# mLSTM cell and squared-ReLU FFN on one core: chunks 5 and 6 in 64x64 quarters, FFN2 of the first group ahead of FFN1 of the third

## The chip, the cores and the metric

One Trainium2 chip, one of its cores. The kernel is one launch; its time is the device time of that core in microseconds (us), given as the median of several runs. The engines are named as the profile names them: PE (TensorE, matmuls; PEld its weight loads), DVE (VectorE), ACT (ScalarE), POOL (GpSimd) and SP (SyncE, which only issues DMAs). All data are float32.

## The reference

Two blocks follow each other. The first is an mLSTM cell: for each of 4 batches and 8 heads a state C (40 x 40) and n (40) is carried over 768 steps of time. The second is a feed-forward network (FFN) with a squared ReLU on the 3072 x 320 result.

```python
batch, n_heads, seq, head_dim = (4, 8, 768, 40)
for t in range(S):
    m_new = np.maximum(f_gate[:, :, t] + m, i_gate[:, :, t])
    f_stab = np.exp(f_gate[:, :, t] + m - m_new)
    i_stab = np.exp(i_gate[:, :, t] - m_new)
    C = f_stab[..., None, None] * C + i_stab[..., None, None] * np.einsum('bhd,bhe->bhde', vt, kt)
    n = f_stab[:, :, None] * n + i_stab[:, :, None] * kt
    h_tilde = np.einsum('bhde,bhe->bhd', C, qt)
    nq = np.einsum('bhd,bhd->bh', n, qt)[:, :, None]
    denom = np.maximum(np.abs(nq), 1.0)
    y[:, :, t] = o * h_tilde / denom            # o = sigmoid(o_gate)
x = attn_out.transpose(0, 2, 1, 3).reshape(3072, 320)
h = np.maximum(x @ w_in, 0.0)                   # w_in 320 x 2048
out = (h * h) @ w_out                           # w_out 2048 x 320
```

## The kernel before

**Chunks.** Time is cut into chunks of 128 steps: 6 for a batch (NB), 24 in all (NT), numbered s = 0 to 23, c = s mod 6 within the batch. "Chunk 5" in the title is s=4, "chunk 6" s=5, "chunk 7" s=6, "chunk 8" s=7; below, and in the prediction, a chunk is named by s. Within a chunk the recurrence is turned into matmuls: scores k q^T (`scores`), weighted by exponentials of the gates (`weigh`, ACT, eight exponentials a chunk, L511; the causal mask is an affine select on POOL, `mask`, L469/L475), times the values (with a column of ones, so that the denominator comes along), plus the old state times q with its decay; the state C of the next chunk is the old one decayed plus k^T times weighted v. Two chunks make a group g of 256 rows for the FFN (12 groups, NG).

**Two forms of the attention.** For s < X_SQ = 6 `attend` works with full 128x128 tiles: old state times q (`hi`, L622), the state's update (`dC`, L634), weighted scores times values (`hp`, L645); then DVE puts them together, and `normalise` (L805 to 818) divides. The 128 rows of x must be turned for the FFN: `turn_rows` (L843 to 853) does it with two transposes (L848) and four half ones (L850) on PE and one ACT copy (L853). From s = 6 on `attend_begin` and `attend_end` do the same products in 64x64 quarters of PE (`values_of_C` L708, `values_of_P` L727, `new_C` L738), in two halves: the first in `attend_begin`, the second in `attend_end`, with a tiny DVE operation (L700) between them that the second half waits for. The numerators come out turned; DVE transposes 32x32 squares of them (L758), they are stored to DRAM (`store_num`, L773) and loaded again in the other order (`load_num`, L778, four DMAs), DVE scales (`normalise_turned`, L790 to 803), the rows are stored (`store_rows`, L828), loaded (`load_rows`, L833, four DMAs) and transposed in squares on DVE (`turn_squares`, L840). k and q are turned likewise by `pair_up` (to DRAM), `load_squares` (L402, four DMAs) and `turn_kq` (L409), from s = KQ_SQ = 7 on; `scale_q` (L672) multiplies q by its decays (`decays`, ACT).

**FFN.** FFN1 of groups 0 and 1 is plain (`ffn1`, four steps, L874 and L885; ACT takes the ReLU and the square, L898 and L904). From group 2 on it is a fast product of the Strassen kind: `ffn1_open` and `ffn1_close` for each of two halves, full blocks by `blocks` (L1041), the last 64 columns of x by `ffn1_rows` in quarters (L1090), sums of blocks on DVE (L1073, L1075, L1108 to L1111). Its sums of w_in (`sums_of_win`) and of x (`sums_of_x`, which needs both chunks of the group turned) are made ahead. FFN2 of group 0 is plain (`ffn2`, 32 matmuls, L911); from group 1 on it is fast (`ffn2_fast`, L965) with sums of w_out (T, `sums_of_weights`, whose fourth part updates w_out in place) and of the squared activations (S, `sums`, L960) made by DVE.

**Rounding.** The weights come in 18 pieces by DMA (`raw`); each is rounded by `words` (ACT, L220 and L222), `join` (DVE, L231 to L236) and an add on POOL (L240) before PE uses it.

**Order.** The order on every engine is written by hand and each engine runs its list in order; so do the queues by which SP and POOL issue DMAs. Up to chunk s = 5 a loop over u = 0 to 7 does for each chunk s = 2 + u // 2: on even u scores, weights for chunk s+1 and one step of FFN1; on odd u attention, `normalise`, the transposes of k and q of the next chunk and another step of FFN1. Then a loop over `parts` runs with n: each entry is a quarter of a part (1, g, i) = FFN1 of group g or (2, g, i) = FFN2, four to a chunk, s = 6 + n // 4, and `at` = n % 4: scores at 0 (of two chunks at a time from s = 8 on), attend at 1, normalising at 2.

```python
parts = [(1, 2, i) for i in range(4)] + [(2, 0, i) for i in range(4)]
for g in range(1, NG):
    parts += [(2, g, i) for i in range(4)]
    if g + 2 < NG:
        parts += [(1, g + 2, i) for i in range(4)]
```

So before, FFN1 of group 2 (n = 0 to 3, chunk 6) runs ahead of FFN2 of group 0 (n = 4 to 7, chunk 7); FFN2 of group 1 begins at n = 8. `ffn1_begin` takes a first piece of FFN1 of group 2 at n = 0.

## Time and profile before

| | |
|---|---|
| median of 6 runs | 492.33 us (490.98 to 494.95) |
| profiled execution | 490.98 us, of which the span is 489.2 |
| PE busy | 481.6 us |
| DVE, ACT, POOL busy | 341.5, 240.6, 216.0 us |
| one step of the plain FFN1: 16 records of L874 and 8 of L885 | 4.6 to 4.8 us |
| one step of the plain FFN2: 16 records of L911 | 4.4 us |
| first scores of chunk 6 (n = 0) | begin at 89.65 us |
| first matmul of FFN2 of group 1 (n = 8) | scores at 129.76, L965 at 130.59 us |

The span runs from the first instruction to the last; 1.78 us lie around it. Rows of the timeline give the start in us, the time of the group, engine, line, operation, output and inputs, and in square brackets the engine's idle time ahead of it with what ended it. In the chain of waits each row is a start, a duration and the work that ended last there. In the waits view a row has the waiting engine and line, what it waited for, the total us, the number and the longest. A row of the windows view gives the stretch, its length, the busy time (and instructions) of PE, PEld, DVE, ACT and POOL, PE's granted clock, the share of the DMA engines and GB/s. Some tens of us at the start belong to the loading of weights and gates.

### The profile page before, as it was taken

Reading aid. Unit: us, or ns where it says so; the run is one execution under the profiler, and the core shown is the slowest. Engines: PE = TensorE matmul, PEld = TensorE weight load, DVE = VectorE, ACT = ScalarE, POOL = GpSimd, SP = SyncE. Lnnn points to the kernel's source line nnn. Section 1 sums busy time; section 2 is a strip of 40 time slices with the busy share of each in tenths; the row PEclk is TensorE's granted clock in tenths of the full one; section 3 lists DMA queues with packets and bytes.
Section 4 is the critical chain, followed back from the end, with each engine's and each line's share of the span. In section 5 each row is a group of like instructions: output and inputs, shape, how many; then the busy total and the mean of one; then the engine's idle time right before and its main releaser. Section 6 shows DMA issues by size and latency. Waiting matters only on the chain.

```text
span 489.2 us, 15237 instructions
## 1 busy us (share of the span) xinstructions
PE 481.6 (98%) x6169; PEld 448.8 (92%) x6169; DVE 341.5 (70%) x704; ACT 240.6 (49%) x531; POOL 216.0 (44%) x322
## 2 busy tenths in 40 slices
PE   9999999999999999999999999999999999999997
PEld 4886788897799999999999999999999999999996
DVE  7899767888956856857866946857956956635441
ACT  4676997764522650942742941742942641513300
POOL 6455533332679178078279078088174040020000
PEclk9999999999999999999999999999999999999999
DMA  9999997745878579669678668758565622200000
GB/s 183 226 240 239 297 230 185 149 86 145 167 131 201 126 128 217 135 117 210 128 121 221 133 107 216 130 105 220 118 105 122 151 54 82 55 29 2 3 27 29
DMA packets 191095, 68.08 MB, mean 139 GB/s; under 512 B 158832, under 2 KB 180240, under 8 KB 191024
## 3 DMA queue, kind: packets, MB, share of 16 engines
q1 hardware_dynamic: 185280, 57.50, 55.7%
q0 software_dynamic: 5600, 9.50, 8.3%
q8 instruction: 49, 0.80, 0.7%
q14 instruction: 22, 0.18, 0.1%
q10 hardware_dynamic: 144, 0.10, 0.1%
HBM read 54.77 MB, written 18.01 MB: 149 GB/s over the span
## 4 chain that ended last, share of the span: by engine, by line
PE 84%; ACT 6%; SPq 4%; DMA 3%; issue 1%; POOL 1%; DVE 0%; POOLq 0%; ACTq 0%
PE h_ps L965 35%; PE h_ps L1041 24%; PE h_ps L1090 7%; PE h_ps L911 4%; PE h_ps L874 3%; PE numT L727 3%; PE numT L708 2%; DMA lent_t<-in_moe_w_in_dram 1%; SPq L210 1%; PE numT L738 1%; PE tp L575 1%; SPq L1151 1%; PE h_ps L575 1%; ACT g_c L511 1%; DMA raw<-in_moe_w_in_dram 1%
## 5 line engine op out<-in xcount | busy, mean ns | idle before, releaser
L475 POOL TENSOR_SCALAR_AFFINE_SELECT A_bc<-A_bc 64x512 f32<-64x512 f32 x32 | 23.2, 725 | 80.5 <-ACT kq L492 57.4
L965 PE MATMUL h_ps<-T,S 128*128 128x160 f32 x352 | 51.7, 300 | 0.6 <-ACT g_c L1107 0.6
L1071 ACT COPY r_sb<-h_ps 128x512 f32<-128x512 f32 x18 | 10.6, 586 | 84.2 <-PE h_ps L1041 84.2
L965 PEld LDWEIGHTS h_ps<-T,S 128*128 128x128 f32 x352 | 48.9, 190 | 1.0 <-ACT g_c L1107 0.8
L965 PE MATMUL h_ps<-w_out,g 128*128 128x160 f32 x336 | 49.2, 303 | 0.0
L981 DVE TENSOR_TENSOR y_sb<-y_sb,h_ps 128x160 f32<-128x160 f32 x44 | 14.1, 320 | 47.9 <-PE h_ps L965 47.8
L965 PEld LDWEIGHTS h_ps<-w_out,g 128*128 128x128 f32 x336 | 46.1, 190 | 1.3 <-issue 0.5
L1041 PE MATMUL h_ps<-xT,w_in 128*128 128x128 f32 x320 | 42.8, 278 | 0.0
L1041 PE MATMUL h_ps<-lent_t,w_in 128*128 128x128 f32 x320 | 42.2, 275 | 0.0
L1041 PEld LDWEIGHTS h_ps<-xT,w_in 128*128 128x128 f32 x320 | 38.9, 192 | 1.4 <-issue 1.0
L1090 PE MATMUL h_ps<-xT,w_in 64*64 64x128 f32 x960 | 39.1, 272 | 0.0
L1041 PEld LDWEIGHTS h_ps<-lent_t,w_in 128*128 128x128 f32 x320 | 38.9, 192 | 0.2 <-issue 0.2
L1041 PE MATMUL h_ps<-lent_t 128*128 128x128 f32 x320 | 39.0, 275 | 0.0
L1041 PEld LDWEIGHTS h_ps<-lent_t 128*128 128x128 f32 x320 | 37.3, 192 | 0.0
L505 ACT ACTIVATE A_bc<-A_bc,b_R 128x64 f32<-128x64 f32 (+1 forms) x128 | 35.7, 362 | 2.7 <-POOL A_bc L475 2.3
L1090 PEld LDWEIGHTS h_ps<-xT,w_in 64*64 64x64 f32 x960 | 34.8, 133 | 1.3
L379 POOL DMA_DIRECT2D va<-in_v_dram x56 | 34.3, 619 | 1.2 <-DMA kq_rows<-in_k_dram 1.1
L758 DVE STREAM_TRANSPOSE tn<-numT 128x256 f32<-128x256 f32 x36 | 14.0, 429 | 28.8 <-PE numT L708 19.5
L874 PE MATMUL h_ps<-xT,w_in 128*128 128x256 f32 x128 | 30.1, 385 | 1.6 <-ACT xT L853 1.0
L1033 POOL TENSOR_TENSOR lent_t<-xT 128x128 f32<-128x128 f32 (+1 forms) x18 | 14.7, 833 | 32.7 <-DVE xT L840 32.7
L874 PEld LDWEIGHTS h_ps<-xT,w_in 128*128 128x128 f32 x128 | 23.4, 190 | 6.0 <-POOL w_in L240 1.8
L965 PE MATMUL h_ps<-w_out,g_c 128*128 128x160 f32 x192 | 28.0, 302 | 0.0
(218 smaller groups left out, 1150.5 us busy)
## 6 DMA issues: line engine op xcount, KB each, us to landing
A_bc<-a_slots SPq DMA_DIRECT2D x32, 256.0 KB, 4.5
num_rows<-tn SPq DMA_DIRECT2D x18, 256.0 KB, 2.2
kq<-num_rows SPq DMA_DIRECT2D x72, 64.0 KB, 2.4
raw<-in_moe_w_out_dram SPq DMA_DIRECT2D x7, 640.0 KB, 5.2
kqT<-kq_rows SPq DMA_DIRECT2D x34, 128.0 KB, 3.7
og<-in_o_gate_dram SPq DMA_DIRECT2D x24, 160.0 KB, 5.0
out_dram<-y_sb SPq DMA_DIRECT2D x24, 160.0 KB, 3.1
raw<-in_moe_w_in_dram SPq DMA_DIRECT2D x7, 512.0 KB, 6.7
```

Source lines behind the costliest of these rows:

```text
L379: eng.dma_start(dst[HALVES[n], PR * (1 - late_keys) : PR * (2 - late_keys)], src[HALVES[late_keys], PR * m : PR * (m + 1)],)
L475: nc.gpsimd.affine_select(part, part, compare_op=ALU.is_ge, fill=-1e30, base=0, pattern=[[0, PR], [0, 2], [1, DP]], channel_multiplier=-1,)
L505: nc.scalar.activation(A[0][:, x, to], A[0][:, x, to], AF.Exp, bias=b_R[:, b, c, own, x : x + 1],)
L727: nc.tensor.matmul(d["numT"][m][HALVES[e], i, t0:], lhsT=va_w[s % NKQ][keys, at * D1 : at * D1 + DP], rhs=rhs, start=(s % NB == 0 and i == ...
L758: nc.vector.transpose(to[:, 2 * m : 2 * m + 2], d["numT"][m].rearrange("p c t -> p (c t)"))
L874: nc.tensor.matmul(hs[i][:, n, :], lhsT=w_in[:, a, fb * P : (fb + 1) * P], rhs=xT[:, :, a, :], start=(n == 0 and a == 0), stop=False,)
L911: nc.tensor.matmul(o_ps, lhsT=st["g2", g][:, fb, j * P : (j + 1) * P], rhs=w_out[:, fb, :], start=(fb == 0), stop=(fb == NF - 1),)
L965: nc.tensor.matmul(to, lhsT=lhsT[:, p], rhs=rhs[:, p, :], start=(start and p == 0), stop=(p == NPAIR - 1), skip_group_check=True,)
L981: add = lambda to, a, b: nc.vector.tensor_tensor(to, a, b, op=ALU.add)
L1033: sub = lambda to, a, b: eng.tensor_tensor(to, a, b, op=ALU.subtract)
L1041: nc.tensor.matmul(to[:, n, :], lhsT=lhsT[:, 4 * q + n, :], rhs=rhs, start=(start and n == 0), stop=True, skip_group_check=True,)
L1090: nc.tensor.matmul(to[cols, n, :], lhsT=w_in2[rows, 4 * q + n, cols], rhs=rhs, start=(start and n == 0), stop=True, skip_group_check=True,)
```

## The change

- X_SQ goes from 6 to 4: chunks 4 and 5 go through `attend_begin`, `attend_end`, the round trips through DRAM and `turn_squares`. They keep the full-size scores and get their state from the full-size form of chunk 3, in its wider layout, at chunk 4. The tile `num` lends its place to their transposed numerators, and the dead halves of other chunks' k and q tiles to their decays and loaded numerators.
- `turn_rows` isn't called for chunks 4 and 5.
- At u = 2 the eight exponentials of chunk 4 (unmasked) and its `decays` are issued ahead of the rounding words; the mask for chunks 4 and 5 is an affine select with fill 0 on the weights (`mask_W`), after the exponentials.
- FFN2 of group 0 (n = 0 to 3, chunk 6) runs ahead of FFN1 of group 2 (n = 4 to 7, chunk 7). `ffn2` holds both accumulators and takes the last two blocks of w_out (14, 15) last; `ffn1_begin` is gone; the scores of chunk 7 stand between the halves of chunk 6's attention; from n = 8 on the list of parts is the same.
- Rounding is done with n = 1 instead of n = 4.
- The loads of k and v of chunks 8 and 9 go from SP (u = 5 and 7) to POOL (n = 2 and 3); `load_o` and `pair_up` move by some steps; `sums_of_win`, `sums_of_weights` and `sums` are placed anew: w_in's at u = 5 and 6 and n = 1, T at n = 3, 4 and 9, the update of w_out at n = 9 (before n = 8), S of group 1 at n = 6, 7, 8 and 9 (before two at 6, then 8 and 9).
- `bdm`, a block mask for chunk 0's state, is replaced by two copies of 64 partitions.

```diff
-    KQ_SQ, X_SQ, ROT = 7, 6, 8
+    KQ_SQ, X_SQ, ROT = 7, 4, 8
...
-        eng = nc.sync if s < 10 else nc.gpsimd
+        eng = nc.gpsimd
...
+    def mask_W(s):
+
+        nc.gpsimd.affine_select(
+            st[s]["W"], st[s]["W"], compare_op=ALU.is_ge, fill=0.0, base=0, pattern=[[0, H], [1, P]],
+            channel_multiplier=-1,
+        )
...
     def decays(s):
 
         if s % NB > 0:
-            e = st[s]["eA"] = kq_b[2 + s % 2][:, 1].rearrange("p (j two) d -> p j (two d)", two=2)
+            home = kq_b[2 + s % 2 if s >= NB else s - X_SQ - 1]
+            e = st[s]["eA"] = home[:, 1].rearrange("p (j two) d -> p j (two d)", two=2)
...
-            if c == 0:
-                nc.vector.tensor_tensor(Cn[:], dC[:], bdm[:], op=ALU.mult)
+            for i in range(2 if c == 0 else 0):
+                nc.vector.tensor_copy(Cn[HALVES[i], :, i, :], dC[HALVES[i], :, i, :])
...
+    F2 = [(j, fb) for half in ((0, 8), (8, 14), (14, 16)) for j in range(GT) for fb in range(*half)]
+
+    def ffn2(step):
+        if step == 0:
+            st["o_ps"] = [ps_h.tile([P, W], F32, name="h_ps")[:, :DM] for _ in range(GT)]
+        for j, fb in F2[8 * step : 8 * step + 8]:
...
-            blocks(X, F11, xT[:, 0, 0, :], q, True)
-            nc.scalar.copy(m1[:], X[:])
+        blocks(X, F11, xT[:, 0, 0, :], q, True)
+        nc.scalar.copy(m1[:], X[:])
...
-    WIN_SUMS = {5: 0, 6: 1, 7: 3}
+    WIN_SUMS = {5: (0, 1), 6: (3,)}
...
-                turn_rows(s - 1)
+                if s - 1 < X_SQ:
+                    turn_rows(s - 1)
                 scores(s)
                 ffn1(u // 4, u % 4)
             if u == 2:
+                weigh(4, masked=True, vw=False)
+                decays(4)
                 rounding.words()
...
             if u == 2:
-                mask(s + 1)
                 rounding.join()
+                mask_W(4)
                 rounding.join()
-                weigh(s + 1, masked=True)
+                values(4)
                 rounding.words()
...
-                weigh(s + 1, masked=(u == 0), vw=(u > 0))
+                weigh(s + 1, masked=(u != 6), vw=(u == 6))
+                if u == 4:
+                    mask_W(5)
                 square_half()
+                if u > 0:
+                    scale_q(s)
...
-            attend(s)
+            if s < X_SQ:
+                attend(s)
+            else:
+                attend_begin(s)
+                attend_end(s)
+                store_num(s)
...
-            for r in {5: (8,), 7: (9,)}.get(u, ()):
-                load(r)
...
+                load_num(s)
             transposes(s + 1, (True, True))
             rounding.words()
             ffn1(u // 4, u % 4)
             square_half()
+            if u == 5:
+                decays(5)
+            if u == 7:
+                normalise_turned(4)
+                store_rows(4)
+                rounding.fetch()
+                rounding.join()
...
-    turn_rows(5)
...
-    parts = [(1, 2, i) for i in range(4)] + [(2, 0, i) for i in range(4)]
-    for g in range(1, NG):
+    parts = []
+    for g in range(NG):
         parts += [(2, g, i) for i in range(4)]
         if g + 2 < NG:
             parts += [(1, g + 2, i) for i in range(4)]
-    LAST = (17, 17, 17, 17, 18)
+    ROUNDED = (17, 18)
...
+        if n == 0:
+            turn_kq(7)
+            pair_up(8)
+            load_rows(4)
+            rounding.words()
+            rounding.join()
...
             do(store_num, s)
+            if n == 1:
+                normalise_turned(5)
+                store_rows(5)
+                turn_squares(4)
             do(load_num, s)
+            if n == 1:
+                load_rows(5)
+                weigh(7, masked=True)
+                sums_of_win(2)
...
-        if 5 <= n < 8:
-            sums_of_weights(n - 5)
-        if n == 6:
-            sums(1, slice(0, NPAIR), (1, 2))
+        if n == 3:
+            load_o(8)
+            load_o(9)
+            sums_of_weights(0)
         if n == 8:
-            sums_of_weights(3)
             sums(1, slice(0, NPAIR), (3,))
         if n == 9:
+            sums_of_weights(3)
             sums(1, slice(0, NPAIR), (4,))
+            sums_of_weights(2)
...
-        if n == 0:
-            ffn1_begin(g)
-            sums_of_x(g)
-            sums_of_win(2)
...
             do(store_rows, s)
+            if n == 2:
+                pair_up(9)
+                load_rows(6)
+                turn_squares(5)
+                sums_of_x(2)
...
+        if n in (2, 3):
+            load(6 + n)
+        if n == 5:
+            load_o(10)
+            load_o(11)
...
+        if n == 4:
+            sums_of_weights(1)
+        if n in (6, 7):
+            sums(1, slice(0, NPAIR), (n - 5,))
```

## What the change should do to the time

> **What bounds the kernel.** I read the totals first, then the waits of TensorE (PE), then the chain that ended last, then single stretches.
>
> ```profile
> span 489.2 us, 15237 instructions
> PE 481.6 (98%) x6169; PEld 448.8 (92%) x6169; DVE 341.5 (70%) x704; ACT 240.6 (49%) x531; POOL 216.0 (44%) x322
> ...
> PE h_ps L874 <- ACT xT L853: 1.0, 1, 1.0
> ...
> PE h_ps L965 <- ACT g_c L1107: 0.6, 1, 0.6
> ...
> PE numT L738 <- DVE kq L700: 0.3, 1, 0.3
> ```
>
> PE is busy for 98% and its waits after the start are three: 1.0, 0.6 and 0.3 us. So from about 60 us on a microsecond of PE work saved is a microsecond of span, unless it turns into a wait. Before 60 us the chain runs through ScalarE (ACT) and the DMA of the weights instead:
>
> ```profile
> 43.48 5.12 DMA raw<-in_moe_w_in_dram
> ...
> 49.93 1.12 ACT g_c L511 x4
> ...
> 51.28 0.98 ACT g_c L511 x3
> ...
> 59.89 0.38 ACT xT L853
> 60.27 0.04 issue
> 60.31 3.72 PE h_ps L874 x16
> ```
>
> ACT waits for weights from about 44.3 to 48.7 us, then does chunk 4's eight exponentials (L511, 2.4 us), and all that follows is late until PE's stall at 60.31. Behind it the chain is PE alone; these are the rows that the change touches:
>
> ```profile
> 65.09 1.05 PE hi L622 x8
> 66.14 0.89 PE dC L634 x8
> 67.04 1.75 PE hp L645 x16
> ...
> 74.21 0.37 PE tp L848 x2
> 74.58 0.37 PE tp L850 x4
> ```
>
> Attention of chunk 4 costs 3.59 us of PE from its first matmul (65.03) to the next work (68.62), chunk 5's 2.70 (80.69 to 83.39: no new state), and each of turn_rows 0.74. In 64x64 quarters the same work of chunk 7 is, in the timeline of PE:
>
> ```profile
> 114.22 0.45 PE L708 MATMUL numT<-kq,C 40*64 40x128 f32 x8
> 114.48 0.62 PE L727 MATMUL numT<-A_bc,va 64*64 64x128 f32 x16
> 114.92 0.39 PE L738 MATMUL numT<-vw,kq 64*64 64x41 f32 x16
> 115.59 0.44 PE L738 MATMUL numT<-vw,kq 64*64 64x41 f32 x16 [0.28 <-DVE kq L700]
> 115.85 0.65 PE L727 MATMUL numT<-A_bc,va 64*64 64x128 f32 x16
> 116.31 0.40 PE L708 MATMUL numT<-kq,C 40*64 40x128 f32 x8
> 116.65 0.54 PE L911 MATMUL h_ps<-w_out,g 128*128 128x320 f32 x1
> ```
>
> Start to start that is 2.43 us, of which some 0.4 is the gap ahead of 115.59, while VectorE (DVE) does L700's tiny operation between the halves.
>
> **The change, part by part.**
>
> Chunk 4 (s=4) in quarters: its begin and end stand next to each other as chunk 7's do above, so it takes 2.43 us, gap included, and 3.59 - 2.43 = 1.16 is saved. Behind a quarter stretch the first full-size matmul is followed later than usual: the next start comes 373 ns after the L911 of 116.65, against 272 elsewhere; so 0.10 is lost and 1.06 remains. Chunk 5 has no L738: 0.26 + 0.44 in begin, 0.46 + 0.34 in end, 0.4 for the gap, 0.1 for the switch, 2.03 in all against 2.70: 0.67.
>
> The Trainium skill speaks against this: TensorEngine Tiling (Array Packing), Tiling Modes, says that changing the tiling mode drains TensorE. The trace agrees and gives the 0.10 above; with each chunk entering and leaving the mode once, the sum by the rule is two such losses, 0.2 us, and by the row the same unless entering costs as much again, 0.4.
>
> turn_rows(4) and (5) go from PE and become DMA round trips: 2 x 0.74 = 1.48 saved on PE. ACT loses two copies (0.46 each), DVE gets two transposes of 0.5.
>
> chunk 4's weigh and decays ahead of the rounding words (u=2): 2.44 + 1.24 = 3.7 us of ACT, and the idle ahead of 48.69 is 4.27 by the timeline of ACT; the chunk's gates (A_bc) landed at 43.76. It fits with 0.6 to spare. ACT then has 2.4 us less behind 49.8 and the 1.24 of decays is new but hidden. PE's gap at 60.31 (1.26 start to start) should go but for 0.1: 1.15. Bounds: 0 if the weights' own arrivals (51.0, 54.0, 55.6, 57.6) hold the chain, 1.26 if all of it goes.
>
> Chunk 7 runs in FFN1(2) now, whose rows (L1090) stand between its halves, so the gap at 115.59 goes: 0.39. FFN1(2) no longer overlaps with rounding; ffn1_begin's matmuls are the same ones in another order, 0. The four FFN2 steps are the same matmuls (4.37 a step before), 0; the two output copies are on ACT, which is half idle, 0. The mask as an affine select on W (POOL, 1.1 each) replaces that on A, one for one, now behind the exponentials instead of ahead: chunk 4's is wanted at 63.8 and its W is there before 53, so 0; without that cover it would put 1.1 between weigh and attend. Chunk 0's state is copied in two halves (0.3 each) where one multiply was, and three memsets go, all ahead of 40 us: 0. Two scale_q (0.65 each) are new on DVE, and normalise_turned (1.85) takes less than normalise did (3.4 for chunk 4, 69.76 to 73.6): 0 while DVE has gaps, as it has up to 90 us (12.46 busy of 15). The last two weight pieces are rounded by n=1 instead of n=4; the final one (DVE 1.84, then POOL 1.55) should be there by 98, and FFN2's fourth step reads it at 102: 0, with 4 us in hand.
>
> SP and POOL: chunk 8's and 9's loads (seven issues each, about 0.62 apiece, 4.4 us a chunk) leave SP for POOL in steps 2 and 3. POOL has 7.5 busy of 19 there (90 to 109 us), so 0; if it had none free, the mask and vw of chunk 7 would be late by 4.4, and they have more than that. SP gets ten new issues for each of chunks 4 and 5 (two stores, eight loads) at 0.35 to 0.45, about 4 us a chunk, in the place of the 14 loads that it lost.
>
> DVE is where it may be paid. The windows by stage:
>
> ```profile
> 109.00:130.00 21.00, 20.72 (x183) 14.63 (x176) 18.99 (x34) 11.71 (x29) 9.27 (x14) 1.00 0.64 144
> ```
>
> The third busy figure is DVE: 18.99 of 21 us already, with FFN2(0) as cover. Now FFN1(2) lies there, whose sums on its blocks (L1073 to L1111: six of 0.6 to 0.7 a half) must keep up with PE, and the S and T sums (1.2 and 1.45 each) that FFN2(1) reads move to steps 3 to 9. I walk it on PE's times of before less the savings: step n=0 starts at 85.3 (89.65 less 4.36) and n=8, FFN2(1), at 125.0 (129.76 less 4.75), in either order of the two parts between. An FFN1 takes 18.1 to 18.5 with its scores (148.5 to 166.6 for group 3), so FFN1(2) starts at about 106.5 and has its first half by 115.8. Chunk 7's numerators leave PE 7.2 behind its start, as chunk 9's did in group 3 (148.51 to 155.7): 113.7; transposes 0.8; the round trip from store to last load landed took 6.1 to 7.5 us for chunks 6, 7 and 9: 120.6 to 122. Then in DVE's order: normalise_turned 1.85, S1 1.2, the four closing sums 2.4, S2 1.2, so S2 at 127.3 to 128.7, and 129.2 with one row stretched. FFN2(1) wants S2 after scores (0.8) and 16 matmuls (2.19): 128.0. A wait of 0 to 1.2, I take 0.7, since stretched rows are common there. The update of w_out (sums_of_weights(3), now at n=9, 1.45) stands behind turn_kq 1.15, weighted 1.0, S3 1.2, the two transposes and C 1.1 and some small ones: about 0.6 behind the second step's use of it, with 0 to 1 as bounds. T2 follows 2.7 later (S4 1.2, itself 1.45) and is wanted one step (4.4) later: 0. Together 1.3.
>
> The start of FFN1(2) needs chunk 5's rows in x: normalised at n=1 (to 95.9), stored and loaded again (3.0 + 3.8 by the shorter round trips), turned and summed (sums_of_x 1.07) by 104.8 in DVE's order, against 107.4 where PE reads the sums (0.9 into FFN1(2)). It is 2.6 early: 0.
>
> Sum: 1.06 + 0.67 + 1.48 + 1.15 + 0.39 - 1.3 = 3.45 us. From the profiled run, 490.98 (span 489.2 and 1.78 around it), that makes 487.5; the median of the six runs, 492.33, is 1.35 above the profiled one, so on the median I expect 488.9.
>
> **Rivals.** 0.5% of the time is 2.46 us, and less than that a measurement of this kernel can't tell from no change: faster is below 489.87, slower above 494.79.
>
> A, no new stalls: all DVE work is in time. Then 4.75 is gained: 487.6. For it: several DVE rows that I count are stretched in before by POOL work beside them (L672 at 124.65 took 1.23 where 0.68 is usual). Against it: the window's 18.99 of 21.
>
> B, DVE becomes the bound of steps 4 to 9: the same stretches fall on the longer list; four rows by 0.55 are 2.2, and both waits grow by up to as much. 1.3 + 1.5 to 1.3 + 3.0 lost: 490.4 to 491.9, within 0.5%. For it: 0.5 us beyond FFN1(2)'s sums is all the slack I find.
>
> C, the gap at 60.31 stays, held by the arrival of the last weights (57.6 us) instead of by weigh: 488.9 + 1.15 = 490.05. For it: DMA share there is 1.10, a full queue. Against it: ACT is busy without a break from 49.8 to 60.3, so it isn't waiting.
>
> D, slower: chunk 5's round trip through DRAM is late. It waits twice for a store's receipt and stands on SP behind chunk 6's store. Its loads were 2.7 to 7.0 us in before (x_rows to xT). At 7.0, and 3.6 for the store, the rows land at 106.5 instead of 102.7. DVE waits in its transpose for them, in order, with T0, the sums of FFN1(2) and S behind it, so PE pays the delay almost whole: 3.8 less the 2.6 in hand at FFN1(2), but all 3.8 at S2: 488.9 + 3.8 = 492.7, no change. From 108.6 on, 5.9 late, it is slower than before; with chunk 6's store ahead of it on SP at 3.4 instead of 2.0 (as num_rows at 157.5) and one issue held for 1.8 instead of 0.5 (as L833's at 155.2) it is 6.5 late: 495.4.
>
> E, that quarters bring nothing since LDWEIGHTS and not matmuls bound them: against it stands chunk 7's own 2.43 us.
>
> **How the numbers follow.** Forecast 0.52 (own range 487.6 to 489.9: both stalls at nothing, or 0.7 + 0.6 grown by 1.0), A and better 0.08, B 0.19, C 0.07, D beyond 494.8 0.14 (with what B may come to if both add up). Faster: nearly all of the forecast, and A, less the part of it on the bound: 0.58. Same: B, C and the rest: 0.28. Slower: 0.14. The range runs from 486.7 (A, and the gaps between begin and end of chunks 4 and 5, 0.4 each, gone as well) to 493.0 (D at 7.0, and a little of C).
>
> **What would show it.** In the profile after: L848 and L850 last for chunk 3; L622/L634/L645 for chunks 4 and 5 replaced by L708/L727/L738 rows of 2.4 and 2.0 us; no wait at the first L874 of the second group's FFN1; step n=0 beginning near 85.3 and FFN2(1) near 125.0; waits of PE on DVE's S and w_out of 0.5 to 1 us each; no wait at FFN1(2)'s opening. Wrong if PE waits for xT or xs at 106, or if DVE's list of steps 5 to 9 runs more than 2 us behind, or if the gap at 60 remains.

## The result, and the profile after

The changed kernel took 495.5 us (median of 21 runs, 492.95 to 498.2), the kernel before 491.95 (47 runs): a ratio of 1.0072 with an interval of 1.0059 to 1.0085. That is 3.5 us slower, where 3.45 faster were forecast; it lies above the range (486.7 to 493.0). The profiled execution took 494.2 us, its span is 492.5. Ratios here and below are over fast runs alone, which leaves out any run more than 1.5% above the fastest of its kernel (three of the 12 of e3, at most two elsewhere).

The page's totals and, from the waits view, the longest waits of PE after:

```profile
span 492.5 us, 15409 instructions
PE 478.9 (97%) x6229; PEld 447.2 (91%) x6229; DVE 343.1 (70%) x719; ACT 242.8 (49%) x534; POOL 226.3 (46%) x335
```

```profile
PE h_ps L980 <- DVE S L975: 4.0, 1, 4.0
PE h_ps L1056 <- issue: 1.7, 1, 1.7
PE tp L870 <- DVE x_sb L840: 1.1, 1, 1.1
PE numT L746 <- issue: 1.0, 1, 1.0
...
PE h_ps L980 <- DVE w_out L961: 0.2, 1, 0.2
```

PE is 2.7 us less busy than before (481.6), so the work was saved; three waits that were not there, 4.0, 1.7 and 1.0 us, took more. The 1.1 stands before 30 us, where the kernel before waits 0.5 at the same place (L848 for x_sb); its 1.0, at 60.3 us, is gone in this execution.

Up to FFN2(1) nearly all came as the prediction walked it. In the timeline of PE, chunk 4 in quarters:

```profile
64.09 0.45 PE L727 MATMUL numT<-kq,Co 40*64 40x128 f32 x8
...
65.47 0.44 PE L757 MATMUL numT<-vw,kq 64*64 64x41 f32 x16 [0.28 <-DVE kq L718]
...
66.52 1.09 PE L553 MATMUL tp<-ident,kq 128*128 128x128 f32 x8
```

66.52 - 64.09 = 2.43, as forecast; chunk 5 took 1.98 (forecast 2.03 with its switch). n=0 began at 85.1 (forecast 85.3), n=8 at 124.64 (forecast 125.0; before 129.76). So 5.1 us were in hand at n=8. That the starts fit so closely is partly luck: in this execution no gap was left at 60 us, but in most profiles of its variants one was (e4, below), and their FFN2(0) began 0.1 to 2.8 us later (86.48 here, 86.6 to 89.3 there). From there to the last matmul it took 364.7 us instead of 355.8: 8.9 more. Comparing the starts of the same matmuls in both traces, stretch by stretch, the 8.9 lie here:

| stretch | more than before, us |
|---|---|
| first step of FFN2(1): wait for S2, then half clock | 5.21 |
| attend of chunk 8, at half clock | 0.67 |
| second step of FFN2(1): update of w_out | 0.47 |
| at 156.6, "issue" | 1.76 |
| at 340.8, "issue" | 1.28 |
| at about 352, where before had a gap of 0.73 | -0.64 |
| the rest | 0.18 |

(The tail behind the last matmul is 0.5 shorter, so the spans differ by 3.3.)

The first row, in the timeline of PE and in the windows (stretch, its length, busy PE, PEld, DVE, ACT, POOL, granted clock, DMA share, GB/s):

```profile
125.41 2.44 PE L980 MATMUL h_ps<-w_out,g 128*128 128x160 f32 x16
131.90 3.35 PE L980 MATMUL h_ps<-T,S 128*128 128x160 f32 x16 [4.04 <-DVE S L975]
```

```profile
124.50:133.00 8.50, 4.46 (x68) 4.18 (x61) 7.71 (x17) 2.71 (x8) 3.22 (x6) 1.00 1.09 177
133.00:137.00 4.00, 4.00 (x58) 3.67 (x60) 2.26 (x4) 4.00 (x8) 0.00 (x0) 0.57 1.00 147
```

PE stands still for 4.04 us, and the clock that it is then granted is 0.57 on the mean of the next 4 us (0.5 from 133.2 to 136.6): the 16 matmuls that take 2.4 us take 3.35. DVE made S2 late. Its timeline:

```profile
113.84 0.78 DVE L780 STREAM_TRANSPOSE tn<-numT 128x256 f32<-128x256 f32 x2 [2.00 <-PE numT L727]
...
125.15 0.17 DVE L812 TENSOR_SCALAR dm<-kq 128x8 f32<-128x8 f32 x1 [3.29 <-DMA kq<-num_rows]
...
127.00 1.22 DVE L975 TENSOR_TENSOR S<-g 128x1024 f32<-128x1024 f32 x1
...
130.53 1.22 DVE L975 TENSOR_TENSOR S<-S,g 128x1024 f32<-128x1024 f32 x1
```

Chunk 7's numerators were turned by 114.6, as walked (114.5), but were back only at 125.03: 10.4 us after they were turned, not 6.1 to 7.5. DVE idled for 3.29 us at the head of its list with S1 and S2 behind. The reason stands in the timeline of SP's queue:

```profile
106.64 0.53 SPq L850 DMA_DIRECT2D x_rows<-x_sb  x1
107.22 1.26 SPq L343 DMA_DIRECT2D kq_rows<-in_k_dram  x2
108.53 1.24 SPq L343 DMA_DIRECT2D kq_rows<-in_q_dram  x2
112.01 3.00 SPq L855 DMA_DIRECT2D xT<-x_rows  x4
115.06 1.10 SPq L413 DMA_DIRECT2D og<-in_o_gate_dram  x2
116.32 1.03 SPq L942 DMA_DIRECT2D out_dram<-y_sb  x2
117.45 0.40 SPq L795 DMA_DIRECT2D num_rows<-tn  x1
120.35 2.77 SPq L800 DMA_DIRECT2D kq<-num_rows  x4
```

SP stands from 109.8 to 112.0 at `load_rows(6)`, waiting for chunk 6's stored rows (issued 106.64, landed 112.00). Those four loads, two o_gate loads and two output stores issue before the store of the numerators, which was ready at 114.6 and issued at 117.45. It landed at 120.28, its loads at 122.2 to 125.0. So the 10.4 us are 2.8 in the queue and 7.6 for the round trip itself, from the issue of the store to the last load landed.

A second queue effect, in the timeline of ACT:

```profile
131.21 0.47 ACT L417 ACTIVATE og<-og 128x320 f32<-128x320 f32 x1 [5.70 <-DMA og<-in_o_gate_dram]
```

`load_o(10)` and `load_o(11)`, moved to n=5, issued at 126.3 and 127.8 behind the numerators' loads and `load_squares(9)` (92.9 and 93.5 before). `half_tanh` waits for them, and behind it in ACT's list stand the FFN's ReLU (L1105), the copy y (L1000), and chunk 9's decays and exponentials.

### The profile page after: what moved, and what is told of

It reads as the page before. It is cut to its first block, busy times and chain, and to the rows that moved or that the text cites. A ratio compares the mean times of both kernels' runs of the same rounds, so it can differ in the third digit from the quotient of the medians.

```text
span 492.5 us, 15409 instructions
## 1 busy us (share of the span) xinstructions
PE 478.9 (97%) x6229; PEld 447.2 (91%) x6229; DVE 343.1 (70%) x719; ACT 242.8 (49%) x534; POOL 226.3 (46%) x335
## 4 chain that ended last, share of the span: by engine, by line
PE 88%; DVE 5%; issue 2%; DMA 2%; ACT 1%; SPq 1%; POOL 0%; DVEq 0%; POOLq 0%
PE h_ps L980 34%; PE h_ps L1056 24%; PE h_ps L1089 7%; PE h_ps L896 4%; PE h_ps L934 4%; PE numT L746 3%; PE numT L727 2%; PE numT L757 1%; PE h_ps L579 1%; PE h_ps L907 1%; PE idle L1138 1%; DMA kqT<-kq_rows 1%; PE tp L579 1%; PE tp L553 1%; DVE mag L231 1%
## 5 line engine op out<-in xcount | busy, mean ns | idle before, releaser
L980 PE MATMUL h_ps<-T,S 128*128 128x160 f32 x352 | 52.7, 304 | 4.1 <-DVE S L975 4.0
L1070 ACT COPY r_sb<-h_ps 128x512 f32<-128x512 f32 x20 | 11.7, 586 | 86.8 <-PE h_ps L1056 86.8
L375 POOL DMA_DIRECT2D va<-in_v_dram x64 | 39.2, 619 | 2.6 <-DMA kq_rows<-in_k_dram 2.5
```

What stands on the lines that cost most here:

```text
L375: eng.dma_start(dst[HALVES[n], PR * (1 - late_keys) : PR * (2 - late_keys)], src[HALVES[late_keys], PR * m : PR * (m + 1)],)
L980: nc.tensor.matmul(to, lhsT=lhsT[:, p], rhs=rhs[:, p, :], start=(start and p == 0), stop=(p == NPAIR - 1), skip_group_check=True,)
```

## Experiments

Each run's ratio is to the kernel before on the same chip, with its interval. "From n=8" is, in the profiled execution, the time from scores of chunk 8 to the last matmul (before 355.8, after 364.7).

**One delay at a time (e1 to e4).**

e1: S1 and S2 of group 1 ahead of chunk 7's numerators on DVE.

```diff
+            if n == 6:
+                sums(1, slice(0, NPAIR), (1, 2))
             do(normalise_turned, s)
...
-        if n in (6, 7):
-            sums(1, slice(0, NPAIR), (n - 5,))
```

> The changed kernel with S1 and S2 of group 1 ahead of normalise_turned(7) on DVE instead of behind it. Theory A (S2 is late only because it is queued on DVE behind the wait of 3.29 us for chunk 7's numerators): both sums (2.4 us) fit into that idle time, the PE stall of 4.2 us at 127.6 goes, and with it the stretch of half clock at 134 (about 1.6 us); 5.8 us faster than the changed kernel, ratio to before about 0.995. Rival B (DVE simply has too much work in these steps): the lateness moves to the closing sums and shows as a PE wait elsewhere; ratio 1.003 or more. Rival C (the low clock there has a cause of its own): the stall goes and the half clock stays; about 0.9985.

Measured 1.0049 (1.0023 to 1.0076), from n=8 362.8. The wait for S2 and the half clock behind it are gone (0.5 us is left there, for DVE's g_c), but 2.3 us came up in chunk 8's attend and 2.9 at 149.8, where PE waits for POOL, POOL's mask for ACT, and ACT 5.9 us for o_gate. So one repair uncovers the next wait.

e2: `load_o(10)` and `load_o(11)` one step later still (`n == 5` becomes `n == 6`).

> The changed kernel with the two loads of o for chunks 10 and 11 one step later, behind the numerators of chunk 7 on SP. Theory A (SP's queue in order holds the store of these numerators back): the store is issued 1.2 us sooner (116.2 instead of 117.45), DVE's idle 3.3 and PE's stall 4.2 shrink by 1.2 each, and the stretch of half clock may shorten; ratio to before 1.002 to 1.005. Rival D (the transfers are slow, whatever is queued): no change, 1.007.

Measured 1.0206 (1.0171 to 1.0242). The loads issued some 6 to 7 us later, ACT idled 11.2 us (5.7 in the changed kernel), and the kernel lost 6 to 7 us more. Not all of that is waiting: PE waits 1.8 and 2.0 us at 138.9 and 155.0, where the changed kernel has no wait, and the granted clock stood at one half for 17.1 us between 128 and 360, against 3.4. The store of the numerators, expected sooner, issued at 117.75 (117.45 in the changed kernel): these two loads stand behind it in SP's queue, not ahead.

e3: POOL's loads of chunks 8 and 9 in n=5 and 6 instead of 2 and 3.

```diff
-        if n in (2, 3):
-            load(6 + n)
+        if n in (5, 6):
+            load(3 + n)
```

> The changed kernel with the loads of k and v of chunks 8 and 9 (14 DMAs on POOL) three steps later. Rival D (these 14 DMAs crowd the DMA engines, so that chunk 6's rows took 5.4 us to land, 106.6 to 112.0, and held up SP): rows land in about 3.2 us, the store of chunk 7's numerators is issued about 2 us sooner, the PE stall shrinks to about 2; ratio 1.000 to 1.004. Theory A in its narrow form (issue times on SP alone): no change in the landing, 1.007.

Measured 1.0025 (0.9995 to 1.0055). Chunk 6's rows landed 4.4 us after their store instead of 5.4, but POOL's traffic then met the numerators (back at 127.8; S2 wait 5.5). In this profile moving POOL's loads only moved the collision, and the store still stood 2.8 us in SP's queue. How much these loads cost in all stays open: the ratio is below the changed kernel's 1.0072, but the medians of all runs, 495.73 and 492.54, differ by 0.65%.

e4: the kernel before with chunk 4's mask and exponentials ahead of the rounding words, alone.

```diff
             if u == 2:
+                mask(s + 1)
+                weigh(s + 1, masked=True, vw=False)
                 rounding.words()
...
-                weigh(s + 1, masked=True)
+                values(s + 1)
```

> The kernel before with only chunk 4's mask and eight exponentials moved ahead of the rounding words. If weigh is what makes the xT copy late: PE's gap of 1.26 us at 60.3 goes, ratio 0.9975. If the weights' arrival holds the chain: ratio 1.000.

Measured 1.000 (0.998 to 1.002); the gap at 60 is still 1.3. In the profiles of the changed kernel and its variants it lay between 0.1 and 1.3, 0.4 less than before on the mean, and the first piece of w_out landed anywhere from 50.2 (the changed kernel) to 54.0 us (e7). So the exponentials' new place is worth nothing that could be measured by itself. That the arrival of the weights holds this chain, as rival C said, fits; no run moved the arrival alone.

**Combinations that leave SP's order alone (e5 to e8).**

e5: the o_gate loads of chunks 8 to 11 at u=7, before the queue fills.

```diff
+            if u == 7:
+                for r in range(8, 12):
+                    load_o(r)
             if u > 4:
                 load_num(s)
...
-            load_o(8)
-            load_o(9)
...
-        if n == 5:
-            load_o(10)
-            load_o(11)
```

> The changed kernel with the loads of o for chunks 8 to 11 at u=7 on SP, in its idle time ahead of chunk 5's load_num, instead of at n=3 and n=5. Theory F (two delays on SP in order: chunk 7's numerators are stored 2.85 us late behind four other DMAs, and the o of chunks 10 and 11 land at 131.5, so that ACT is blocked 5.7 us in half_tanh and everything behind it): the block on ACT goes, the store of the numerators comes 1.05 us sooner, the wait on S2 shrinks from 4.2 to about 3.2 and stays the bound; ratio to before 1.002 to 1.005. Rival G (only the order of DVE matters, not SP): no change, 1.007.

e6 is e5 with e1's edit; e7 is e5 with the two output stores of FFN2(0) on POOL (`nc.gpsimd.dma_start` at L942); e8 has all three.

> Both: o of chunks 8 to 11 at u=7 and S1 and S2 ahead of normalise_turned(7). Theory F: neither delay has a wait of PE behind it any more; the waits of e1 (0.7 + 0.5 + 1.2 + 2.8 around 130 to 150 us) shrink to 1 in all; 4 us less than e1, ratio 0.995 to 0.997. Rival G: e1's waits stay, 1.005.

> As e5, and the two stores of FFN2(0)'s result issued by POOL instead of SP; S1 and S2 where the change has them. Theory F: the store of chunk 7's numerators comes 2.2 us sooner than in the changed kernel (115.3), DVE's idle of 3.3 shrinks to about 1.1 and PE's wait for S2 from 4.2 to about 2, and with a shorter wait the stretch of half clock goes; ratio 0.997 to 1.000. Rival G: 1.005.

> All three edits. Theory F: as e6 or 0.5 us better, ratio 0.993 to 0.997: the prediction's 488.9 nearly reached. If POOL's two more DMAs or another wait takes it back: like e6 or worse.

Measured 1.005 (1.0021 to 1.008), 1.006 (1.0031 to 1.009), 1.004 (1.0014 to 1.0066), 1.0032 (1.0006 to 1.0058). ACT's wait is gone in all four, and e5's profiled execution (490.5 us, from n=8 358.5) shows what the change could be; but the median of its runs is 495.7. The store of chunk 7's numerators still issued at 119 in e5, behind chunk 6's rows, whose store took 5.3 to 6.2 us to land. Removing issues near it (e7) didn't help: the store still issued 2.3 us after the numerators were turned (2.0 in e5), since SP waits for the rows, not for its own issue time.

**SP's order (e9 to e11).** e9 changes only this: `load_rows(6)` goes behind chunk 7's numerators (nobody needs these rows before n=11), its `turn_squares(6)` to n=8.

```diff
                 pair_up(9)
-                load_rows(6)
...
             do(load_num, s)
+            if n == 5:
+                load_rows(6)
```

> The changed kernel, with the loads of chunk 6's normalised rows (8 transfers on SyncE) issued after chunk 7's numerators are loaded again instead of ahead of chunk 7's attend, and their DVE transpose moved behind S(3) of the second FFN2; nobody needs these rows before the fourth group's input sums. Nothing else of the queue is touched: the four o_gate loads, the two stores of the first FFN2's output and load_squares(9) stay. Theory (the queue's wait for x_rows(6) is what holds chunk 7's numerators): store_num(7) issues within 1 us of the transposes of its numerators plus the four issues that still stand ahead of it, about 115 to 116 on the profile's clock in place of 117.5; reload landed by 122 to 123; the PE wait for S2 in the first step of FFN2(1) falls from 4.2 us to below 1.5, and no half clock follows it: 5 us from n=8 on come back, of which 1 to 2 are lost again because o_gate 10 and 11 still come late and hold ACT; ratio to the kernel before 0.998 (0.995 to 1.002). Rival (it is the number of transfers in flight, not the queue's order): store_num(7) earlier, but its reload lands at 124 to 125 as before, ratio 1.006.

e10 is e9 with e5's edit, e11 is e10 with the update of w_out moved:

```diff
         if n == 9:
-            sums_of_weights(3)
...
             sums_of_weights(1)
+        if n == 5:
+            sums_of_weights(3)
```

> As e9_rows_late, and all o_gate loads of chunks 8 to 11 issued in the win stage, before the queue is full (as in e5_og_early). Theory of two separate costs: e5_og_early left a wait of 1.2 us for S2 and 119.1 for store_num(7); here store_num(7) issues at 115 to 117, S2's wait is below 0.5, ACT is not held by o_gate: ratio 0.996 (0.993 to 1.000). Rival (the spare time is gone everywhere and any two DMA-bound waits return elsewhere): ratio 1.003 as in e8_all_three.

> As e10_og_early_rows_late, and the in-place update of w_out (B12, line 961) moved from the second FFN2's second step to the fifth step of the loop (first of FFN1(2)'s closes), where DVE is idle for 2 us. Theory: of the wait at the second FFN2's second step (0.5 us where S2 was late, 1.2 to 2.1 where S2 came in time) nothing is left: 0.5 to 1.5 us faster than e10, ratio 0.994 (0.991 to 0.998). Rival: DVE's later work slides by the same amount and the wait comes back as one for S4 (line 975): same as e10.

Measured 1.0084 (1.0058 to 1.0111), 1.0046 (1.003 to 1.0062), 1.0015 (0.9996 to 1.0035). e9's timeline of SP's queue, then its waits of PE from 125 to 165 us, then a row of DVE:

```profile
117.72 0.38 SPq L795 DMA_DIRECT2D num_rows<-tn  x1
120.00 1.75 SPq L800 DMA_DIRECT2D kq<-num_rows  x4
```

```profile
PE h_ps L1056 <- POOL lent_t L1051: 1.5, 1, 1.5
PE h_ps L980 <- issue: 1.4, 1, 1.4
PE numT L727 <- DVE A_bc L601: 1.0, 1, 1.0
PE h_ps L980 <- DVE S L975: 0.6, 1, 0.6
```

```profile
132.52 1.25 DVE L405 STREAM_TRANSPOSE kqT<-kqT 128x1024 f32<-128x1024 f32 x1 [2.21 <-DMA kqT<-kq_rows]
```

In e9 all of PE ran 2.0 us later (n=8 at 126.6), yet the numerators were back at 123.5, 6.9 us after they were turned instead of 10.4, and the wait for S2 is 0.6 instead of 4.0. The store's time in the queue fell from 2.8 to 1.1 us and the round trip from 7.6 to 5.8. So the place of `load_rows(6)` on SP's queue made that wait; how much of it by holding the queue and how much by its own transfers beside the round trip, e9 doesn't separate. In the eight variants that keep `load_rows(6)` in front (e1 to e3, e5 to e8, e14) the store stood 2.0 to 3.2 us in the queue and the round trip took 5.6 to 9.1; in e10 to e13 and e15 the store issued at once, and S2 is 0 to 1.0 us late.

The total didn't gain, for other waits took its place. 1.8 us went at 150.9, where PE waits for POOL, POOL for ACT, and ACT 6.1 us for the o_gate loads (issued 128.5 and 130.2). Chunk 8's attend took 2.4 us more than before; 1.3 of that is a wait for A_bc behind the DVE row above, which waits for `load_squares(9)`, and those loads the edit itself put behind `load_rows(6)`. Two gaps without a semaphore, 1.6 us at 138 and 1.7 at 341, the second with half clock behind it, are the subject of the last three runs. The expectation for e9 allowed 1 to 2 us for o_gate and was too small. In e10, where o_gate is early too, POOL's wait is gone and that for A_bc is 0.3. So delays hid behind each other, and repairing one alone gains little or nothing (e1, e5, e9). In time the row loads' share isn't shown by itself: e10 differs from e5 by them, and 1.0046 can't be told from 1.005.

**DVE's part (e12, e13).** Both start from e11, in which S2 is still 1.0 us late. e12 puts S1 and S2 into DVE's last gap:

```diff
             sums_of_weights(1)
+            sums(1, slice(0, NPAIR), (1, 2))
...
-        if n in (6, 7):
-            sums(1, slice(0, NPAIR), (n - 5,))
```

> As e11_og_rows_w, and the second FFN2's S1 and S2 (1.22 us each on DVE) moved from behind chunk 7's numerators to the place right behind T1 in the loop's fourth step, where e11's DVE waits 2.1 us for chunk 7's attend (114.4 to 116.5 on its clock). In e11 DVE is busy from 117 to 141 almost without a break and S2 ends 1.2 us late. Theory (with SyncE's queue and o_gate out of the way DVE is what the second FFN2 waits for): the wait for S2 is gone, S(3) and S4 come 2 us sooner, n=8 starts at most 0.4 us later; ratio 0.998 (0.994 to 1.001). Rival (the transposes of chunk 7's numerators are now late behind S1 and S2, and the reload with them): n=8 unchanged, a new wait of 1 us or more on POOL's or ACT's products of chunk 8, ratio 1.001 to 1.004.

Measured 1.0023 (1.0005 to 1.0041). The timelines of DVE and PE in e12:

```profile
114.62 1.22 DVE L975 TENSOR_TENSOR S<-g 128x1024 f32<-128x1024 f32 x1
115.87 1.79 DVE L975 TENSOR_TENSOR S<-S,g 128x1024 f32<-128x1024 f32 x1
117.69 0.16 DVE L718 TENSOR_SCALAR kq<-numT 1x1 f32<-1x1 f32 x1
```

```profile
117.91 0.44 PE L757 MATMUL numT<-vw,kq 64*64 64x41 f32 x16 [1.87 <-DVE kq L718]
```

S2 is in time, and PE pays 1.87 us earlier instead, waiting for the tiny L718 between the halves of chunk 7's attend, now behind S1 and S2. n=8 came at 130.5 instead of 127.9, which neither theory said.

e13 takes work out of the stretch: the transpose of chunk 4's rows from n=1 to n=2, T0 from n=3 to n=2, the update of w_out from n=5 to n=4.

> As e11_og_rows_w, with DVE's work moved to where it idles and nobody is queued behind it: the transpose of chunk 4's rows (which holds DVE for 3.0 us at 97.9 to 100.9 on e11's clock, waiting for x_rows) goes to the loop's third step, next to chunk 5's; T0 (1.49 us) goes from the fourth step to the third, ahead of chunk 6's section; the in-place update of w_out (1.45 us) goes to the fourth, behind T1. Theory (DVE's queue is the bound of this stretch once SyncE's queue and the o_gate loads are out of the way): the 2.9 us of T0 and of the update leave the stretch between chunk 6's section and S2, S2 comes 1 us or more sooner, its wait falls from 1.2 to below 0.4, no new wait in front: ratio 0.998 (0.995 to 1.001). Rival (what bounds S2 then is the landing of chunk 7's numerators at 124.1, so S2 comes at most 1.2 us sooner, and POOL's loads, 3 us sooner as well, push chunk 6's or 7's numerators back by as much): ratio 1.001 to 1.004 as before.

Measured 1.0017 (0.9988 to 1.0046). S2's end moved only from 4.1 to 3.7 us behind n=8. DVE's timeline in e13, the first closing sum of FFN1(2)'s first half and S2:

```profile
119.28 0.69 DVE L1106 TENSOR_TENSOR r_sb<-r_sb,h_ps 128x512 f32<-128x512 f32 x1 [0.91 <-PE h_ps L1056]
...
130.57 1.22 DVE L975 TENSOR_TENSOR S<-S,g 128x1024 f32<-128x1024 f32 x1
```

From 119.28 to the end of S2 at 131.79 DVE is busy for 12.26 of 12.51 us (e11: from 118.49 to 132.04, 13.31 of 13.55). The work taken out made this stretch 1.0 us shorter, but it began 0.8 us later: the first closing sum waits for PE, and PE came later, by waits of 0.6 and 0.8 us at 108 and 110 for the turned rows and their sums on DVE, where the moved transpose now stands, and by L718, now behind the update of w_out. So what is left of S2's wait is DVE's full list behind the first closing sum, in the order that it has; neither side named what took the gain back.

**The gaps that no semaphore explains (e14 to e16).** The page of the changed kernel counts the packets by which PE's program arrives:

```profile
q8 instruction: 49, 0.80, 0.7%
```

49 packets of 16384 bytes, 256 instructions of 64 bytes each: 12,544, for 12,640 recorded PE instructions. Take every gap of PE over 0.45 us behind 120 us that ends less than 1.9 us after such a packet has landed, in the changed kernel and e1 to e13, and count PE's instructions from the start. There are 28; one is a wait for DVE, and the other 27 all stand at 188 to 193 modulo 256 (the expectation of e14 had counted 17). Some of them, and the one gap of the kernel before, which stands elsewhere and which its profile puts down to ACT's g_c:

```
run     gap at   gap, us   ends after packet landed, us   instruction   modulo 256
after    156.6     1.85      1.53                            3265          193
after    340.8     1.12      1.46                            8897          193
e6       137.8     2.00      1.46                            2753          193
e7       158.1     1.97      1.35                            3265          193
e8       136.5     2.46      1.34                            2753          193
e9       341.4     1.74      1.46                            8892          188
e11      137.8     1.42      1.49                            2749          189
e13      156.1     1.10      1.63                            3261          189
before   351.8     0.73      1.12                            9174          214
```

The Trainium skill, Advanced Engine Details and Errata, ISA Cache, says that the sequencers cache their instructions in lines of 16 KB, 256 instructions each. The packets and the places modulo 256 agree. That PE can stand at the edge of a line is read from the gaps above.

The change made the program of PE 128 instructions longer (12,512 to 12,640 recorded), half a line. e14 is the changed kernel with 64 more pairs of weight load and matmul in the first 6 us, where PE runs idle matmuls until the first loads land; e15 is e11, e16 the kernel before, each with the same edit:

```diff
-    def idle(n):
+    def idle(n, w=W):
...
-                t[:], lhsT=zeros[:, :1].to_broadcast([P, P]), rhs=zeros[:, :1].to_broadcast([P, W]), start=True, stop=True,
+                t[:, :w], lhsT=zeros[:, :1].to_broadcast([P, P]), rhs=zeros[:, :1].to_broadcast([P, w]), start=True, stop=True,
...
-    idle(12)
+    idle(4)
+    idle(72, 64)
```

> The changed kernel with 64 more pairs of weight load and matmul on PE in its first 6 us, where PE runs idle matmuls while it waits for the first loads (8 wide idle matmuls give way to 72 narrow ones; nothing else moves). Why: PE's program comes in packets of 16384 bytes on the DMA queue that carries instructions, 49 of them for some 12,600 PE records, 256 instructions each; every PE gap of over 0.5 us that no semaphore explains ends 1.1 to 1.8 us after such a packet has landed, and all of them stand at the same place modulo 256 of the program (188 to 193 in 17 gaps of the changed kernel and its variants). Theory (the change lengthened PE's program by 128 instructions ahead of the second FFN2, so that block edges came to stand around the attends at 137, 156 and 340): with 128 instructions more the edges stand as in the kernel before, the gaps of 1.85 us at 156.6 and 1.1 us at 340.8 are gone and one of at most 0.7 us at about 352 comes back; the wait for S2 stays (4 us and the half clock): 2 to 3 us faster than the changed kernel, ratio to before 1.002 (1.000 to 1.005). Rival (these gaps belong to a place of the kernel, a busy memory or a PSUM wait, and the packets only come along): gaps stay at 156 and 340, ratio 1.007 (1.006 to 1.009).

> e11_og_rows_w (o_gate loads early, chunk 6's row loads late, the update of w_out early) with the same 64 pairs more at the start. Theory: of e11's gaps those at block edges go (1.42 us at 137.8, 0.55 at 156.7, 0.4 at 337), about 0.6 us comes back at 352: 1 to 2.5 us faster than e11, ratio 0.998 (0.995 to 1.000), the first version ahead of the kernel before. Rival: unchanged, ratio 1.0015 (0.9996 to 1.0035 as measured).

> The kernel before with the same 64 pairs more at the start, nothing of the change in it. Theory: its block edges now stand where those of the changed kernel stand: gaps of 0.5 to 2 us appear at about 153 to 156 and 335 to 340 (perhaps at 137), its 0.73 us gap at 351.8 goes: 1 to 3 us slower, ratio 1.004 (1.001 to 1.007). Rival (edges don't matter, or before's DMA traffic leaves the packets in time): no gap over 0.5 us there, ratio 1.000 (0.998 to 1.002); a ratio of 1.000 could also come with the 64 pairs costing up to 1 us at the start, which the start of the loop's first step shows.

| | ratio (interval) | n=8 at | from n=8 | gaps at edges behind n=8, us |
|---|---|---|---|---|
| e14 | 1.0029 (1.0004 to 1.0055) | 126.5 | 361.4 | none |
| e15 | 0.9943 (0.9918 to 0.9969) | 128.2 | 357.3 | none (e11: 1.42 and 0.55) |
| e16 | 1.0019 (0.9996 to 1.0041) | 131.7 | 359.5 | 1.84 at 340.3 |

In e14 the gaps at 156 and 340 are gone, and the one at 352 did not come back; a wait of 2.8 us for S2 and the half clock behind it remain. e15 is the first version faster than the kernel before: median 490.37 us against 492.95 on its chip. (e11 ran on another chip; the two ratios are compared, not the times.) Its waits of PE:

```profile
PE h_ps L980 <- DVE S L975: 1.0, 1, 1.0
PE numT L757 <- DVE kq L718: 0.5, 2, 0.3
...
PE h_ps L1056 <- issue: 0.4, 1, 0.4
```

e16 got the gap at 340, at the same instruction modulo 256 (192) as the changed kernel, and lost its own at 352, but had none at 137 or 156; its time can't be told from no change. So the place of the edge decides where a gap can be, not that it comes; what else it takes stays open. That a packet is delayed by full DMA engines (mean share 0.94 from 155 to 158.5 us and 1.06 from 339 to 343 in the changed kernel) fits, but no run varied that alone.

## Why the prediction was wrong

**Right.** Chunk 4 in 2.43 and chunk 5 in 1.98 us, turn_rows 1.48, n=0 and n=8 to 0.4 us (partly by luck, since the gap at 60 happened to be gone), and no wait at the opening of FFN1(2). The wait for the update of w_out: 0.6 said, 0.47 measured.

**The step that failed** is "the round trip from store to last load landed took 6.1 to 7.5 us for chunks 6, 7 and 9: 120.6 to 122". It took a duration from traces in which the store issued at once (117.58 before, less than 0.1 behind DVE), and never listed what stands ahead of it on SP in the new order. "about 4 us a chunk, in the place of the 14 loads that it lost" counted issue time and set it at 0; what cost was a wait in that queue, `load_rows(6)` for its store, ahead of the numerators. Measured: 2.8 us in the queue, 2.8 for the store to land and 4.8 from there to the last load, 10.4 in all, and S2 4.0 late instead of 0.7 (e9: back to 0.6 with the row loads moved). The round trip itself, 7.6, came at the upper end of what was taken; the term that was missing is the queue. Rival D had this mechanism, two receipts and SP's order, but at chunk 5's rows, where there was slack; that its price, 495.4, came close is luck.

**Not priced at all:** the move of `load_o(10)` and `load_o(11)`, 33 us later on a queue that now waits. It is hidden behind S2's wait in the changed kernel and costs 0.4%, 1.9 us, once that is repaired (e9's ratio against e10's), or more when it grows (e2). And the length of PE's program: 1.76 + 1.28 = 3.0 us of the 8.9; with the edges moved the ratio falls from 1.0072 to 1.0029, 2.1 us (e14, whose wait for S2 was also shorter, 2.8 instead of 4.0). The 0.64 at 352 isn't the edge's: it did not come back in e14.

**Mis-sized:** the gap at 60, 1.15 said, 0 in e4 and about 0.4 on the mean of the changed kernel and its variants. The last rounding of the weights, forecast by 98, ended at 102.3; it cost nothing in the changed kernel's profile, but PE waited 0.4 to 0.8 us for it in e6, e11, e12 and e15. A wait was counted as its own length; after 4.0 us PE also ran for 3.4 us at half clock, 1.8 us more (0.67 in the attend, 1.1 in the first step).

**Rival B**, DVE as the bound, holds for what is left: in e11 and e15 S2 is 1.0 us late with the numerators back in time, since DVE is busy almost without a break ahead of it (e11, e13), and the gap before that stretch is not free (e12). S2 ahead of the closing sums, on e11, wasn't tried.

On sums: the 3.45 forecast less 1.15 is 2.3, and e15, with most of the causes above removed, gained 2.6 between the medians. This is no check of the sum: in the profiled executions e15's span is only 0.5 us shorter than before's (488.7 and 489.2), and its n=8 stands at 128.2, not at 125.0.

## What to carry to other kernels

When steps move, write down the whole list of a DMA queue around each transfer that somebody waits for, with the waits in it: one load that waits for its own store holds everything behind it, and a queue that is cheap in issue time can still be 3 us late. When a repair gains nothing, look for a second delay that was hidden behind the first before giving up the theory: e9 made S2's wait 0.6 us and gained nothing, with e5's edit it stood at 1.0046, with the update of w_out moved at 1.0015. The largest step came last and from elsewhere, 1.0015 to 0.9943 by 64 idle pairs (e15). In this kernel moving the 256-instruction edges gained 2.1 us (e14) and 3.5 (e15) or nothing that could be told (e16), so gaps "issue" are compared modulo 256, and a few idle matmuls at the start are a cheap test.

## What was not expected of the hardware

- Waits at edges of instruction lines: PE stands for 0.5 to 2.5 us and goes on 1.1 to 1.8 us after the packet has landed.
- The clock can fall after a short stop: to 0.5 for 3.41 us after stops of 4.0 (after), 2.8 (e14), 2.3 (e8) and 1.7 us (e16, 340.5 to 342.24, then half clock from 343.15 to 346.57), and for 6.83 us around stops of 4.6 (e2) and 5.5 (e3). It did not fall after 3.0 us in e7 (131.6 to 134.6), 2.7 in e1 and 1.9 in e12, so the length of the stop alone doesn't decide. The Trainium skill, TensorE: Matmul & The Clock Gate, Part 1, tells of a free-running window of 3.4 us; the stretches of 3.41 agree with its length. Its rule, no idle gaps of PE over about 3.4 us, differs from the 1.7 us in e16, and here the measurement decides.
- A store of 192 KB of rows took 5.3 to 6.2 us to land while POOL's 14 loads ran (4.4 without them, e3); the store of chunk 7's numerators, 256 KB, took 2.0 to 3.5 in the same runs.
